# Attention cut into units of 32 queries and 64 keys: two transposes a block, sixteen small products each for scores and outputs, one tile of two banks

## The chip, the cores and the metric

The program runs on one core of one Trainium2 chip. The metric is device time in microseconds (us), the median of 3 runs. Engines are called as in the profile: PE is TensorE (PEld its weight loads), DVE is VectorE, ACT is ScalarE, POOL is GpSimd, SP is SyncE, which here issues most of the loads.

## The reference, cut to what matters

Three stages follow each other: attention with two kinds of mask, a chain of four products, and a mixture of 8 experts to which tokens are assigned in order of their logits. The change touches the attention alone.

```python
# q, k, v: (4, 8, 576, 64), f32
scores = q @ k.T / sqrt(64)
rel = pos[:, None] - pos[None, :]
# heads 0..3: 0 <= rel < 32;  heads 4..7: 0 <= rel < 128 and rel % 4 == 0
scores = where(mask, scores, -1e9)
attn = exp(scores - max); attn = attn / (sum + 1e-9)
x = attn @ v                                  # (2304, 512)
x = (((x @ w1) * (x @ w2)) @ w3) @ w_out
logits = x @ w_gate                           # then each token to one expert, 288 a expert
out[tokens of e] = relu(x @ e_w1[e]) @ e_w2[e]
```

A query sees 32 keys at most. For heads 4 to 7 the launch sorts positions by their remainder of 4, and then these heads have the same band of 32 keys.

## The kernel before

**Blocks.** The attention runs over 36 blocks, 9 for each of 4 batches (`NB`). A block is 64 queries of each of 8 heads with the 96 keys that they can see. In blocks 0 to 7 of a batch all 64 queries belong to one stretch of positions; the ninth (`t % 9 == 8`) collects what is left over of the sorted heads, with its own mask and extra keys and values (`ke`, `ve`).

**One block on each engine.** `att_qk` makes the scores on PE: 8 products of 64 queries by 96 keys over 64 rows, into two banks of PSUM, one for even and one for odd heads (`par`). Every f32 product is two matmuls in the trace. `att_max` (DVE, L193) adds the mask and takes the maximum, four instructions of 128x96. `att_exp` (ACT, L200) makes four exponentials with their sums. `att_norm` divides (two small DVE instructions, then one POOL product of 128x384, L207). `att_tr` turns the block with four PE transposes (L213) into a bank called `tr`, `h` or `ab`; `att_pt` copies it out (ACT, L217). `att_av` makes the outputs with 8 products of 96 keys (L228, in the ninth block also L231) into the bank `rt`. `att_out` writes the rounded value `xh` (two ACT copies, L251 and L252) and the rest `xl` (two DVE subtractions, L253 and L254).

**What runs beside it.** `moe(b)` makes the two products of a batch with w1 and w2 (L477 to L479, three matmuls for each f32 pair, 12 to a product), and `narrow12` and `narrow3` turn the 64-bit weights into f32 on DVE (L135, L137, L139), ACT (L121) and POOL (L124). The attention is a generator; the loop at the end of the listing pulls a step of it after so many dozens of matmuls (`ATT_RATE`, `RUSH`, `FIRST`), so the order of every engine's instructions is fixed by this code. Each engine takes its instructions in order.

**Two phases.** Up to block 17 (`ALONE`) a step of the generator is a single block: the PE gets, without a matmul of `moe` between them, the transposes of block t-2, the outputs of block t-3 and the scores of block t+1. From block 18 on a step takes two blocks: outputs of two, transposes of two, scores of two, then 36 matmuls of `moe`. Batch b needs the blocks of its own eight full positions; the ninth blocks of all batches go into `XT`, which batch 3 reads first.

**Tiles.** PSUM has 8 banks: 4 `ab` (the accumulators of `moe`), 2 `h`, 1 `tr`, 1 `rt`. The scores of the first 7 blocks take `ab` and their transposes `h`; later scores take `h`. A tile is given out again when all that read it are done. Loads: `qk_load` (320 KB a block) is issued three to four blocks ahead, `v_load` (192 KB) one ahead, both by SP, with the 1 MB weight loads in the same row. Eight semaphores stand for the loads in turn, so a load waits until the eighth before it has landed.

Of the kernel before, what the change touches and what calls it, by code (L numbers as in the profile page):

```python
# [21 lines left out]
QB, KB, NB = 64, 96, 9  # L22
HT = 288
# [64 lines left out]
def body(tc, qk_d, v_d, ke_d, ve_d, msk_d, cst_d, tri_d, w1_d, w2_d, w3_d, wo_d, wg_d, e1_d, e2_d, out):  # L88
    nc = tc.nc
    stacks = {}  # L90

    def pool(name, **kw):
# [4 lines left out]
    ps = pool("ps", space=PSUM)  # L97
    wp = pool("wp")
# [4 lines left out]
    bank = lambda shape, tag, dt=F32: ps.tile(shape, dt, tag=tag, name="ps_" + tag,  # L103
                                              bufs={"ab": 4, "h": 2, "tr": 1, "rt": 1}[tag])
# [39 lines left out]
    msk = pa.tile([128, 3, KB], F32, name="msk")  # L144
# [14 lines left out]
    def v_load(t):  # L159
        V[t] = pa.tile([KB, 512], F32, tag="v", name="v", bufs=4)  # L160
        nc.sync.dma_start(V[t], v_d[t // NB, t % NB])
        if t % NB == NB - 1:
            VE[t] = pa.tile([KB, 256], F32, tag="ve", name="ve", bufs=1)
            nc.sync.dma_start(VE[t], ve_d[t // NB])

    def att_qk(t, s=None):
        x = QK.pop(t)
        q = x[:, :256].rearrange("p (i q) -> p i q", i=4)
        k = x[:, 256:].rearrange("p (i q) -> p i q", i=4)

        s = SC[t] = s or [bank([128, 2, KB], "h" if t >= EARLY else "ab") for _ in range(2)]
        ke = KE.pop(t, None)
        for j in range(2):
            for par in range(2):
                r = slice(par * 64, par * 64 + 64)
                for i in (2 * j, 2 * j + 1):
                    p0 = i % 2 * 64
                    if ke is None or j == 0:
                        mm(s[par][p0:p0 + 64, j, :], q[r, i, :], k[r, i, :], start=True, stop=True)
                        continue  # L180
                    for a, key in enumerate((k[r, i, :], ke[r, i - 2, :])):
                        mm(s[par][p0 + 32 * a:p0 + 32 * a + 32, j, :], q[r, i, 32 * a:32 * a + 32], key,
                           start=True, stop=True)

    def att_max(t):
        s = SC.pop(t)
        j = t % NB
        m = 2 if j == 8 else int(j < 4)
        p = pa.tile([128, 4, KB], F32, tag="p", name="p", bufs=4)
        sm = pa.tile([128, 4, 4], F32, tag="sm", name="sm", bufs=4)  # L190
        for i in range(4):
            n = m if i % 2 else int(j == 0)
            dve.tensor_tensor_reduce(p[:, i, :], s[i // 2][:, i % 2, :], msk[:, n, :], scale=-0.125, scalar=1e9, op0=OP.add,  # L193
                                     op1=OP.min, accum_out=sm[:, 1, i:i + 1])
        P[t] = p, sm
# [7 lines left out]
    def att_norm(t):  # L203
        p, sm = P[t]
        dve.tensor_scalar(sm[:, 3], sm[:, 2], 1e-9, None, op0=OP.add)  # L205
        dve.reciprocal(sm[:, 3], sm[:, 3])
        nc.gpsimd.tensor_tensor(p, p, sm[:, 3, :, None].to_broadcast([128, 4, KB]), op=OP.mult)  # L207

    def att_tr(t, tag):
        p = P.pop(t)[0]  # L210
        o = TR[t] = bank([KB, 4, 128], tag)
        for i in range(4):
            nc.tensor.transpose(o[:, i, :], p[:, i, :], ident)  # L213

    def att_pt(t):
        pt = OT[t] = pa.tile([KB, 4, 128], F32, tag="pt", name="pt", bufs=2)
        act(pt, TR.pop(t), AF.Copy)  # L217

    def att_av(t, o=None):
        pt, v, ve = OT.pop(t), V.pop(t), VE.pop(t, None)  # L220
        o = AV[t] = bank([128, 4, QB], "rt") if o is None else o
        for i in range(4):
            for par in range(2):
# [3 lines left out]
                if ve is None or i < 2:  # L227
# [6 lines left out]
    def att_out(t):  # L234
# [11 lines left out]
        def dilated(x):  # L246
            if j == 8:
                return x[:, 2:4, w].rearrange("p h (i c) -> p h c i", c=4)
            return x[:, 2:4, t0:t0 + 253:4]
        od = o[:, 2:4].rearrange("p h (c i) -> p h c i", c=4) if j == 8 else o[:, 2:4]  # L250
        act(xh[:, 0:2, w], o[:, 0:2], AF.Copy)  # L251
        act(dilated(xh), od, AF.Copy)  # L252
        dve.tensor_tensor(xl[:, 0:2, w], o[:, 0:2], f32(xh)[:, 0:2, w], op=OP.subtract)  # L253
        dve.tensor_tensor(dilated(xl), od, dilated(f32(xh)), op=OP.subtract)  # L254

    def attention():

        for t in range(ALONE):
# [18 lines left out]
        qk_load(ALONE + 3)  # L277
        yield done - 1
# [3 lines left out]
        while done < NT:  # L282
            new = list(range(t, min(t + 2, NT)))
            t += 2
            if turned:
                o = bank([128, len(turned), 4, QB], "rt")
                for i, x in enumerate(turned):
                    att_av(x, o[:, i])
            for x, tag in zip(ready, ("tr", "ab")):
                att_tr(x, tag)  # L290
            if new:
# [3 lines left out]
                for x in (t + 2, t + 3):  # L295
                    if x < NT:
                        qk_load(x)
# [216 lines left out]
    nc.sync.dma_start(msk[:, :2], msk_d[:, :2])  # L514
# [6 lines left out]
    while nxt < 4:  # L521
# [4 lines left out]
        if i == 9:  # L526
            nc.sync.dma_start(msk[:, 2:], msk_d[:, 2:])
# [5 lines left out]
    for b in range(B):  # L533
        if b == 3:
            stacks.pop("pa").close()
            p2 = pool("p2")
# [623 lines left out]
    for name in ("p4", "p2", "pm", "xp", "wp", "ps", "dram", "cst"):  # L1160
# [58 lines left out]
```

## Time and profile before

| | |
|---|---|
| Median of 3 runs | 732.63 us (732.27 to 733.89) |
| Profiled execution | 730.56 us |
| its span | 728.8 us, 15964 instructions |
| PE busy in the span | 699.4 us (96%), mean granted clock 0.985 |
| DVE, ACT, POOL busy | 411.4 us, 352.7 us, 264.4 us |

The profiled execution is 1.76 us longer than its span and 2.07 us below the median. A row of the trace names the line of the kernel, the engine, the operation, the tile written and the tiles read, and the sizes; `xN` is the number of instructions that it stands for. Times of matmuls overlap: the start of the next row tells when PE went on, and the duration includes the way through the array.

### The profile page before, as it was taken

How to read it: one execution, taken by the hardware profiler on the slowest of the kernel's cores; microseconds unless marked ns; L12 is line 12 of the kernel's file. 1: busy time of each engine (PE TensorE's matmuls, PEld its weight loads, DVE VectorE, ACT ScalarE, POOL GpSimd, SP SyncE). 2: the span in 40 equal slices, each digit the busy share in tenths (PEclk: the TensorE clock that was granted, in tenths of full speed). 3: DMA queues.
4: the chain of work that ended last, by engine and by line, in shares of the span. 5: the costliest groups of instructions: out<-in, count | busy, mean ns of one | idle time of the engine just before them, and what ended most of it. 6: DMA issues, size and time to landing. Idle time of an engine off the chain costs nothing.

```text
span 728.8 us, 15964 instructions
## 1 busy us (share of the span) xinstructions
PE 699.4 (96%) x6081; PEld 608.9 (84%) x6081; DVE 411.4 (56%) x1414; ACT 352.7 (48%) x812; POOL 264.4 (36%) x305
## 2 busy tenths in 40 slices
PE   4799999999999999999999999999999999999996
PEld 3599778888889988687787878799999999999995
DVE  4879777773321011177886677779687862234321
ACT  5676444555422123333454565355565657655432
POOL 2858421321100035344445253421414145654521
PEclk9599999999999999999999999999999999999998
DMA  8995787971024300111799999768888898996311
GB/s 292 330 298 166 250 324 276 333 262 60 29 73 159 112 5 1 64 60 15 124 137 154 164 151 229 136 201 219 218 265 212 212 246 239 285 274 194 114 33 33
DMA packets 59596, 126.66 MB, mean 174 GB/s; under 512 B 13696, under 2 KB 29440, under 8 KB 56960
## 3 DMA queue, kind: packets, MB, share of 16 engines
q1 hardware_dynamic: 27232, 89.46, 37.0%
q0 software_dynamic: 29696, 31.46, 25.6%
q10 hardware_dynamic: 2592, 4.72, 1.9%
q8 instruction: 48, 0.79, 0.4%
q14 instruction: 28, 0.23, 0.1%
HBM read 87.87 MB, written 15.73 MB: 142 GB/s over the span
## 4 chain that ended last, share of the span: by engine, by line
PE 79%; DVE 7%; issue 6%; ACT 3%; POOL 3%; DMA 1%; POOLq 0%; SPq 0%; DVEq 0%; ACTq 0%
PE ps_ab L477 10%; PE ps_ab L478 9%; PE ps_ab L479 9%; PE ps_ab L623 4%; PE ps_h L1044 3%; PE ps_ab L624 3%; PE ps_ab L625 3%; PE ps_h L1045 3%; PE ps_h L1046 3%; PE ps_ab L1068 3%; PE ps_ab L1069 3%; PE ps_ab L1070 3%; PE ps_rt L821 3%; PE ps_rt L228 2%; PE ps_ab L592 2%
## 5 line engine op out<-in xcount | busy, mean ns | idle before, releaser
L207 POOL TENSOR_TENSOR p<-p,sm 128x384 f32<-128x384 f32 x36 | 45.7, 1280 | 120.5 <-DVE sm L205 74.4
L1068 PE MATMUL ps_ab<-hh,w 128*128 128x288 f32 x248 | 75.8, 306 | 0.0
L1070 PE MATMUL ps_ab<-hh,w 128*128 128x288 f32 x248 | 73.0, 294 | 0.0
L1069 PE MATMUL ps_ab<-hl,w 128*128 128x288 f32 x248 | 73.0, 294 | 0.0
L507 POOL DMA_DIRECT2D wbl<-g x36 | 48.4, 1675 | 63.1 <-ACT wbl L505 54.0
L1056 ACT ACTIVATE hh<-ps_h 128x288 fp32r<-128x288 f32 x62 | 25.6, 413 | 89.3 <-PE ps_h L1046 82.2
L1057 DVE SCALAR_TENSOR_TENSOR hl<-ps_h,hh 128x288 fp32r<-128x288 f32 x62 | 28.3, 456 | 64.7 <-ACT hh L1056 57.0
L200 ACT ACTIVATE p<-p,sm 128x96 f32<-128x96 f32 x144 | 52.0, 363 | 24.8 <-DVE sm L193 23.9
L482 ACT ACTIVATE a<-ps_ab 128x512 f32<-128x512 f32 (+1 forms) x44 | 22.9, 522 | 81.7 <-PE ps_ab L479 74.0
L623 PE MATMUL ps_ab<-Wx,wbh 128*128 128x512 f32 x144 | 59.7, 415 | 0.0
L624 PE MATMUL ps_ab<-Wx,wbh 128*128 128x512 f32 x144 | 56.3, 391 | 0.0
L625 PE MATMUL ps_ab<-Wx,wbl 128*128 128x512 f32 x144 | 56.2, 390 | 0.0
L477 PE MATMUL ps_ab<-x,wah 128*128 128x512 f32 (+1 forms) x144 | 54.8, 381 | 0.7 <-ACT x L251 0.7
L477 PE MATMUL ps_ab<-x,wbh 128*128 128x512 f32 (+1 forms) x144 | 54.5, 378 | 0.0
L478 PE MATMUL ps_ab<-x,wah 128*128 128x512 f32 (+1 forms) x144 | 53.4, 370 | 0.1
L479 PE MATMUL ps_ab<-x,wal 128*128 128x512 f32 (+1 forms) x144 | 53.2, 370 | 0.0
L478 PE MATMUL ps_ab<-x,wbh 128*128 128x512 f32 (+1 forms) x144 | 53.2, 369 | 0.0
L479 PE MATMUL ps_ab<-x,wbl 128*128 128x512 f32 (+1 forms) x144 | 53.2, 369 | 0.0
L484 DVE TENSOR_TENSOR g<-a,ps_ab 128x512 f32<-128x512 f32 (+1 forms) x36 | 22.4, 624 | 53.5 <-PE ps_ab L479 50.6
L1068 PEld LDWEIGHTS ps_ab<-hh,w 128*128 128x128 f32 x248 | 46.8, 189 | 0.0
L1069 PEld LDWEIGHTS ps_ab<-hl,w 128*128 128x128 f32 x248 | 46.7, 188 | 0.1
L1070 PEld LDWEIGHTS ps_ab<-hh,w 128*128 128x128 f32 x248 | 46.5, 188 | 0.0
(296 smaller groups left out, 2041.2 us busy)
## 6 DMA issues: line engine op xcount, KB each, us to landing
est<-e_dram SPq DMA_DIRECT2D x53, 512.0 KB, 5.5
w<-w_dram SPq DMA_DIRECT2D x16, 1024.0 KB, 9.0
qk<-qk_dram SPq DMA_DIRECT2D x36, 320.0 KB, 4.1
w<-est POOLq DMA_DIRECT2D x20, 512.0 KB
wbl<-g POOLq DMA_DIRECT2D x28, 256.0 KB
v<-v_dram SPq DMA_DIRECT2D x36, 192.0 KB, 6.8
kept<-f SPq DMA_DIRECT2D x12, 512.0 KB, 4.8
rows<-e_dram SPq DMA_DIRECT2D x11, 512.0 KB, 4.5
```

The costliest lines, as they stand in the source:

```text
L200: act(p[:, i, :], p[:, i, :], AF.Exp, bias=sm[:, 1, i:i + 1], scale=-1.0, accum_out=sm[:, 2, i:i + 1])
L207: nc.gpsimd.tensor_tensor(p, p, sm[:, 3, :, None].to_broadcast([128, 4, KB]), op=OP.mult)
L477: mm(a, wh[:, k, fs], xh[:, k, ts], start=(k == 0), stop=False)
L478: mm(a, wh[:, k, fs], xl[:, k, ts], start=False, stop=False)
L479: mm(a, wl[:, k, fs], xh[:, k, ts], start=False, stop=(k == 3))
L507: nc.gpsimd.dma_start(x, src, accum_op=OP.add)
L623: mm(a, h[:, f, :], wh, start=(f == 0), stop=False)
L624: mm(a, h[:, f, :], wl, start=False, stop=False)
L625: mm(a, l[:, f, :], wh, start=False, stop=(f == 7))
L1068: mm(y, wh[:, f % 2, ds_], h, start=(f == 0), stop=False)
L1069: mm(y, wh[:, f % 2, ds_], l, start=False, stop=False)
L1070: mm(y, wl[:, f % 2, ds_], h, start=False, stop=(f == end))
```

## The change

A block of 64 queries and 96 keys becomes two units of 32 queries and 64 keys (`UQ`, `UK`): unit u has the queries 32u to 32u+31 and the keys 32u to 32u+63 of the block. The ninth block of a batch stays as it was, with 96 keys.

- Scores: 16 products of 32 queries by 64 keys in place of 8 of 64 by 96. The four head pairs stand in four groups of 32 partitions, the unit in the free dimension.
- Mask, exponentials and division work on 128x64 and 128x256 in place of 128x96 and 128x384.
- Two transposes of 128x128 in place of four of 128x96; the copy `pt` is 128x256 in place of 96x512.
- Outputs: 16 products over 64 keys, 32 columns each, in place of 8 over 96 keys with 64 columns. Unit u uses the keys' rows 64u to 64u+63 and writes bank u.
- The banks `tr` and `rt` become one tile of two banks (`ps_t`, one buffer) that holds the outputs of one or two blocks and the transposes of one or two others. The outputs stand ahead of the transposes on PE in the single steps too. Transposes no longer use `h` and `ab`. From batch 3 on the two banks are `tr` and `rt` again (`psb`).
- The values of a block are loaded by two loads of 64 rows (128 KB each) in place of one of 96 rows; the mask by four small loads that ACT issues and two POOL copies.
- From block 18 on the ninth block (26 and 35) has a step for itself, so there is one step more.

```diff
-    bank = lambda shape, tag, dt=F32: ps.tile(shape, dt, tag=tag, name="ps_" + tag,
-                                              bufs={"ab": 4, "h": 2, "tr": 1, "rt": 1}[tag])
+    def bank(shape, tag, dt=F32):
+        return (psb if tag in ("tr", "rt") else ps).tile(shape, dt, tag=tag, name="ps_" + tag,
+                                                         bufs={"ab": 4, "h": 2, "tr": 1, "rt": 1}[tag])
...
+    def mask_loads():
+        for g in range(4):
+            nc.scalar.dma_start(mku[UQ * g:UQ * g + UQ, 0:2], msk_d[:UQ, 0:2, :UK])
+        for g in range(2):
+            nc.gpsimd.tensor_copy(mku[64 * g:64 * g + 64, 2], mku[64 * g:64 * g + 64, g])
...
     def v_load(t):
-        V[t] = pa.tile([KB, 512], F32, tag="v", name="v", bufs=4)
-        nc.sync.dma_start(V[t], v_d[t // NB, t % NB])
-        if t % NB == NB - 1:
+        V[t] = pa.tile([128, 512], F32, tag="v", name="v", bufs=4)
+        if not last(t):
+            for u in range(2):
+                nc.sync.dma_start(V[t][UK * u:UK * u + UK], v_d[t // NB, t % NB][UQ * u:UQ * u + UK])
+        else:
+            nc.sync.dma_start(V[t][:KB], v_d[t // NB, t % NB])
...
+        if not last(t):
+            for u in range(2):
+                for i in range(4):
+                    for par in range(2):
+                        r = slice(par * 64, par * 64 + 64)
+                        mm(s[par][UQ * i:UQ * i + UQ, u, :UK], q[r, i, UQ * u:UQ * u + UQ], k[r, i, UQ * u:UQ * u + UK],
+                           start=True, stop=True)
+            return
...
+    def turn_bank():
+        return psa.tile([128, 2, 512], F32, tag="t", name="ps_t", bufs=1)
...
-        o = TR[t] = bank([KB, 4, 128], tag)
-        for i in range(4):
-            nc.tensor.transpose(o[:, i, :], p[:, i, :], ident)
+        o = TR[t] = o[:, u, 256:].rearrange("p (x q) -> p x q", x=2)
+        for i in range(2):
+            nc.tensor.transpose(o[:, i, :], p[:, 2 * i:2 * i + 2, :].rearrange("p u k -> p (u k)"), ident)
...
+        if not last(t):
+            o = AV[t] = o[:, :, 128 * n:128 * n + 128].rearrange("p u (i q) -> p u i q", i=4)
+            for i in range(4):
+                for u in range(2):
+                    for par in range(2):
+                        h = 2 * i + par
+                        mm(o[par * 64:par * 64 + 64, u, i, :], v[UK * u:UK * u + UK, h * 64:h * 64 + 64],
+                           pt[UK * u:UK * u + UK, par, UQ * i:UQ * i + UQ], start=True, stop=True)
+            return
...
             if t >= 2:
-                att_tr(t - 2, "tr" if t - 2 >= EARLY else "h")
+                o = turn_bank()
+                if t >= 3:
+                    att_av(t - 3, o)
+                att_tr(t - 2, o)
                 att_pt(t - 2)
-            if t >= 3:
-                att_av(t - 3)
             v_load(t + 1)
...
-            new = list(range(t, min(t + 2, NT)))
-            t += 2
-            if turned:
-                o = bank([128, len(turned), 4, QB], "rt")
+            new = list(range(t, min(t + (1 if last(t) else 2), NT)))
+            t += len(new)
+            if turned or ready:
+                o = turn_bank()
                 for i, x in enumerate(turned):
-                    att_av(x, o[:, i])
-            for x, tag in zip(ready, ("tr", "ab")):
-                att_tr(x, tag)
+                    att_av(x, o, i)
+                for i, x in enumerate(ready):
+                    att_tr(x, o, i)
...
-    nc.sync.dma_start(msk[:, :2], msk_d[:, :2])
+    mask_loads()
```

The order of instructions on PE, first at a single step (outputs of block 7, transposes of block 8 are told by their counts; names are tiles, `C` the identity matrix, `pt` the turned block), before and then of the change:

```order
L479 MATMUL ps_ab<-x,wbl 128x256
L213 MATMUL ps_tr<-C,p 96x128 x4
L228 MATMUL ps_rt<-pt,v 64x64 x8
L179 MATMUL ps_h<-qk 64x96 x8
L477 MATMUL ps_ab<-x,wah 128x256
```

```order
L533 MATMUL ps_ab<-x,wbl 128x256
L266 MATMUL ps_t<-pt,v 64x32 x16
L247 MATMUL ps_t<-C,p 128x128 x2
L195 MATMUL ps_h<-qk 32x64 x16
L531 MATMUL ps_ab<-x,wah 128x256
```

The outputs now stand first, so the transposes no longer run ahead of them; both write the one tile `ps_t`.

On PE where a step takes two blocks (outputs of 18 and 19 and what follows them), before and then of the change:

```order
L479 MATMUL ps_ab<-x,wal 128x512
L228 MATMUL ps_rt<-pt,v 64x64 x16
L213 MATMUL ps_tr<-C,p 96x128 x4
L213 MATMUL ps_ab<-C,p 96x128 x4
L179 MATMUL ps_h<-qk 64x96 x16
L477 MATMUL ps_ab<-x,wbh 128x512
```

```order
L533 MATMUL ps_ab<-x,wal 128x512
L266 MATMUL ps_t<-pt,v 64x32 x32
L247 MATMUL ps_t<-C,p 128x128 x4
L195 MATMUL ps_h<-qk 32x64 x32
L531 MATMUL ps_ab<-x,wbh 128x512
```

The order is the same here; the counts are doubled for the products and halved for the transposes.

On PE at the end of the attention (`xt` is what the ninth blocks write), before: the outputs of the last blocks, then 30 matmuls of batch 2 with 512 columns, of which the first stands here, and only then `xt` is read:

```order
L228 MATMUL ps_rt<-pt,v 64x64 x12
L231 MATMUL ps_rt<-pt,v 64x32
...
L231 MATMUL ps_rt<-pt,ve 64x32
L477 MATMUL ps_ab<-x,wbh 128x512
L478 MATMUL ps_ab<-x,wbh 128x512
```

and of the change:

```order
L277 MATMUL ps_t<-pt,v 64x64 x4
L280 MATMUL ps_t<-pt,v 64x32
...
L280 MATMUL ps_t<-pt,ve 64x32
L531 MATMUL ps_ab<-xt,wah 128x256
L532 MATMUL ps_ab<-xt,wah 128x256
```

The outputs of block 35 have moved behind all of batch 2, and the first matmul after them reads `xt`, to which they belong.

## Rows read from the trace of the kernel before

**Rows 1.** The page: busy time and instructions by engine; PE's instruction queue q8.

```profile
PE 699.4 (96%) x6081; PEld 608.9 (84%) x6081; DVE 411.4 (56%) x1414; ACT 352.7 (48%) x812; POOL 264.4 (36%) x305
...
q8 instruction: 48, 0.79, 0.4%
```

**Rows 2.** Two stretches: length, busy us of PE, PEld, DVE, ACT, POOL, clock, DMA share.

```profile
28.90:104.50 75.60, 72.55 (x798) 62.14 (x796) 60.46 (x194) 42.93 (x161) 41.65 (x40) 0.96 0.81 262
104.50:213.50 109.00, 108.87 (x994) 88.59 (x994) 60.47 (x238) 51.03 (x196) 21.74 (x18) 1.00 0.51 177
```

**Rows 3.** PE's waits: who, for whom; us in total, times, longest.

```profile
PE ps_ab L179 <- DMA qk<-qk_dram: 9.7, 5, 4.0
PE ps_h L179 <- ACT pt L217: 2.4, 2, 1.8
```

**Rows 4.** PE in time, one step of two blocks: start, duration, what.

```profile
121.68 1.15 PE L228 MATMUL ps_rt<-pt,v 96*64 96x64 f32 x32
122.76 0.64 PE L213 MATMUL ps_tr<-C,p 128*96 128x128 f32 x4
123.24 0.60 PE L213 MATMUL ps_ab<-C,p 128*96 128x128 f32 x4
123.77 0.89 PE L179 MATMUL ps_h<-qk 64*64 64x96 f32 x32
124.59 0.50 PE L477 MATMUL ps_ab<-x,wbh 128*128 128x512 f32 x1
```

**Rows 5.** PE in time, scores of a ninth block: matmuls of 64*32 tiles.

```profile
80.78 0.27 PE L182 MATMUL ps_h<-qk 64*32 64x96 f32 x1
...
80.83 0.27 PE L182 MATMUL ps_h<-ke,qk 64*32 64x96 f32 x1
80.89 0.24 PE L182 MATMUL ps_h<-qk 64*32 64x96 f32 x1
...
81.10 0.50 PE L477 MATMUL ps_ab<-x,wah 128*128 128x512 f32 x1
```

**Rows 6.** PE in time, the last outputs, with products of 32 columns.

```profile
211.66 0.39 PE L478 MATMUL ps_ab<-x,wbh 128*128 128x512 f32 x1
211.88 0.39 PE L479 MATMUL ps_ab<-x,wbl 128*128 128x512 f32 x1
212.20 0.92 PE L228 MATMUL ps_rt<-pt,v 96*64 96x64 f32 x24
212.95 0.31 PE L231 MATMUL ps_rt<-pt,v 96*64 96x32 f32 x4
...
213.54 0.50 PE L477 MATMUL ps_ab<-x,wbh 128*128 128x512 f32 x1
```

**Rows 7.** PE in time, a single step; in brackets its wait.

```profile
59.53 0.60 PE L213 MATMUL ps_tr<-C,p 128*96 128x128 f32 x4
60.38 0.69 PE L228 MATMUL ps_rt<-pt,v 96*64 96x64 f32 x16 [0.25 <-PE ps_tr L213]
```

**Rows 8.** DVE in time, beside that step.

```profile
59.89 0.39 DVE L254 TENSOR_TENSOR x<-ps_rt,x 128x128 fp32r<-128x128 f32 x1
```

**Rows 9.** ACT and DVE in time, after the last outputs.

```profile
213.65 0.28 ACT L251 ACTIVATE x<-ps_rt 128x128 fp32r<-128x128 f32 x1 [2.10 <-PE ps_rt L231]
...
214.45 0.38 DVE L254 TENSOR_TENSOR x<-ps_rt,x 128x128 fp32r<-128x128 f32 x1
```

**Rows 10.** DMA queues and issues of the first 60 us: packets, size, us to landing.

```profile
DMA packets 6151, 17.48 MB, mean 291 GB/s; under 512 B 992, under 2 KB 1600, under 8 KB 5120
...
v<-v_dram SPq DMA_DIRECT2D x14, 192.0 KB, 9.3
```

**Rows 11.** A stretch at the lower clock, columns as in rows 2.

```profile
35.20:38.50 3.30, 3.30 (x32) 2.85 (x29) 3.02 (x14) 1.94 (x10) 2.55 (x3) 0.50 1.01 331
```

**Rows 12.** PE in time there: 12 matmuls of 256 columns and what follows.

```profile
35.87 0.58 PE L477 MATMUL ps_ab<-x,wbh 128*128 128x256 f32 x1
...
38.60 0.60 PE L213 MATMUL ps_h<-C,p 128*96 128x128 f32 x4
```

More of the change, by code (lines that the diff above doesn't have):

```diff
@@ L141, in steps64, with last @@
         yield
-    msk = pa.tile([128, 3, KB], F32, name="msk")
+    msk = pa.tile([128, 2, KB], F32, name="msk")
+    mku = pa.tile([128, 3, UK], F32, name="mku")
+    def mask_loads():
[3 more added lines that the diff above has]
+            nc.gpsimd.tensor_copy(mku[64 * g:64 * g + 64, 2], mku[64 * g:64 * g + 64, g])
+    def last(t):
+        return t % NB == NB - 1
     C = cst.tile([128, C_END], F32, name="C")
@@ L187, in att_max @@
         j = t % NB
-        m = 2 if j == 8 else int(j < 4)
-        p = pa.tile([128, 4, KB], F32, tag="p", name="p", bufs=4)
+        w = KB if last(t) else UK
+        p = pa.tile([128, 4, w], F32, tag="pw" if last(t) else "p", name="p", bufs=1 if last(t) else 4)
         sm = pa.tile([128, 4, 4], F32, tag="sm", name="sm", bufs=4)
         for i in range(4):
-            n = m if i % 2 else int(j == 0)
-            dve.tensor_tensor_reduce(p[:, i, :], s[i // 2][:, i % 2, :], msk[:, n, :], scale=-0.125, scalar=1e9, op0=OP.add,
+            m = msk[:, i % 2] if last(t) else mku[:, 0 if i % 2 or j >= 4 else 2 if j else 1]
+            dve.tensor_tensor_reduce(p[:, i, :], s[i // 2][:, i % 2, :w], m, scale=-0.125, scalar=1e9, op0=OP.add,
                                      op1=OP.min, accum_out=sm[:, 1, i:i + 1])
@@ L244, in att_out, with spots @@
         t0 = 256 * (j // 4) + j % 4
[L246 to L254, printed above, removed]
+        if last(t):
+            def spots(x):
+                return x[:, 0:2, w], x[:, 2:4, w].rearrange("p h (i c) -> p h c i", c=4)
+            ins = o[:, 0:2], o[:, 2:4].rearrange("p h (c i) -> p h c i", c=4)
+        else:
+            def spots(x):
+                return [y.rearrange("p h (u q) -> p h u q", u=2) for y in (x[:, 0:2, w], x[:, 2:4, t0:t0 + 253:4])]
+            ins = [o[:, :, i:i + 2].rearrange("p u i q -> p i u q") for i in (0, 2)]
+        for x, y in zip(spots(xh), ins):
+            act(x, y, AF.Copy)
+        for x, y, z in zip(spots(xl), ins, spots(f32(xh))):
+            dve.tensor_tensor(x, y, z, op=OP.subtract)
     def attention():
@@ L294, in attention @@
                     att_qk(x, [y[:, i] for y in o])
-                for x in (t + 2, t + 3):
-                    if x < NT:
-                        qk_load(x)
+                while loaded < min(t + 4, NT):
+                    qk_load(loaded)
+                    loaded += 1
             yield done
@@ L526, in body @@
         if i == 9:
-            nc.sync.dma_start(msk[:, 2:], msk_d[:, 2:])
+            for n in range(2):
+                nc.sync.dma_start(msk[:, n], msk_d[:, 2 * n])
             nc.sync.dma_start(wg, wg_d)
@@ L1159, in body @@
         pass
-    for name in ("p4", "p2", "pm", "xp", "wp", "ps", "dram", "cst"):
+    for name in ("p4", "p2", "pm", "xp", "wp", "psb", "ps", "dram", "cst"):
         stacks[name].close()
```

32 lines of the change are left out of this document (24 added, 8 removed).

## The prediction

> **What bounds the kernel now.** I read the page's busy times first: PE works 699.4 of 728.8 us, DVE 411.4, ACT 352.7, POOL 264.4 [rows 1]. Then the stretches in which attention runs. From 104.5 to 213.5 us, where blocks go two to a step, PE is busy 108.87 of 109.00 us [rows 2]; nothing but PE time counts there, and what PE saves ends up in the total. From 28.9 to 104.5, with single blocks, PE is busy 72.55 of 75.60 us, but DVE 60.46 as well [rows 2]: PE's order is mostly the limit, and here and there it meets a late DVE. Before that the start is a chain with loads in it: PE waited 9.7 us in 5 waits for `qk`, and 2.4 us in 2 waits for the copy `pt` that frees a bank `h` [rows 3]. In the first 60 us the DMA engines move 291 GB/s [rows 10]; their busy share there is about full, 1.01 in the stretch of rows 11. After 213.5 us attention is over; the rest keeps its work and moves as one piece, so gains and losses carry over one to one.
>
> **The change part by part.** The unit is a step of two blocks: outputs from 121.68, transposes from 122.76 and 123.24, scores from 123.77, `moe` again at 124.59 [rows 4], together 2.91 us.
>
> *Transposes.* The second four make the stretch 0.48 us longer (123.24 less 122.76) [rows 4]. Four of eight go: -0.48 us a step of two, -0.24 a block.
>
> *Scores.* Two blocks are 32 matmuls now, four side by side, and take 0.82 us [rows 4]; less 0.17 us from the last start to the next work (80.93 is the last start, 81.10 the next row) [rows 5] that is 8 rounds of 0.08 us for 96 columns. They become 64 matmuls in 8 rounds of eight. The ninth block has this shape, 64*32: eight start within 0.05 us (80.78 to 80.83), the second eight 0.11 us after the first [rows 5]. With 64 columns a round should take two thirds of 0.08, 0.055 us, just above the 0.05 in which eight start. Then 0.11 + 6 x 0.055 + 0.05 + 0.17 = 0.66 us, -0.16 a step; at 0.11 a round, the one gap that the trace has for eight, 0.99 us, +0.17. I take -0.16, since four rounds side by side go at 0.08 with more columns.
>
> *Outputs.* 32 matmuls, two side by side, take 1.08 us [rows 4]: less 0.15, 16 rounds of 0.058 us. The products of 32 columns in the last outputs take 0.59 us for 16 (212.95 to 213.54) [rows 6], 8 rounds of 0.055: half the columns save nothing. The change has 64 matmuls, four side by side, again 16 rounds. I take 0; from -0.05 up to +0.35, if a round of four takes the 0.08 us of the scores.
>
> So a step of two loses 0.64 us, 2.91 to 2.27. After 104.5 us there are 8 pairs of transposes and 7 of scores left: 8 x -0.48 + 7 x -0.16 = **-4.9 us**.
>
> *The step more.* Blocks 26 and 35 ran with a neighbour; each now has runs of its own. A run of outputs, transposes and scores more costs three times the 0.15 to 0.17 us in which nothing starts, and 0.09 for going from `moe` to outputs (0.32 us from 211.88 to 212.20 in place of 0.22) [rows 6]: **+0.6 us**.
>
> *The last block.* The outputs of block 35 now stand right ahead of the matmuls that read `xt`. After the last outputs PE could go on at 213.54 [rows 6]; ACT began at 213.65 and DVE ended the second subtraction at 214.83 [rows 9]. Of these 1.3 us a first matmul of 0.12 fills something, and it needs ACT's copies alone: 0.4 to 1.2 us, **+1.1 us** taken, for the second matmul needs what DVE writes. What hid this before were 30 matmuls of batch 2.
>
> *Single steps.* Two transposes fewer and half of the scores' gain are -0.32, the extra change from `moe` to outputs +0.09: -0.23 us a step. Six such steps lie between 61.6 and 104.5: -1.4. But outputs, now first, wait for the tile that the block before has not left: one buffer, which DVE's subtraction ends. At 59.53 PE had transposes to do and then waited 0.25 us for DVE's L254, which ended at 60.28 [rows 7, 8]; now the transposes stand behind that wait, and such a step gets 0.2 to 0.3 us longer. Two of the four steps from 46 to 61.6 are like that, which leaves 0 for these four. For the six later ones I count half of the gain, **-0.7 us** (0 to -1.4), since DVE is busy 80% there [rows 2].
>
> *Loads.* A block's values come in two loads of 128 KB in place of one of 192. Of 14 in the first 60 us [rows 10] 12 are ordinary blocks: 0.8 MB, at 291 GB/s 2.7 us of DMA time where DMA is full; behind each extra load on SP stand `qk` and the weight loads, and scores wait for `qk`. Against that, the two waits on `h` (2.4 us) [rows 3] lose their cause, as transposes leave `h`, and exponentials, masks, the POOL product and the copy shrink by a third to a half. I take **+0.3 us**, from -3.8 (below) to +2.7. Later loads have time: PE shows no wait on them. Mask loads on ACT and the POOL copies lie ahead of the first scores, at zero; ACT and DVE have nothing else to do then.
>
> *More instructions.* 12162 PE instructions come in 48 packets of q8 [rows 1], 253 each; an ordinary block gets 60 more, 1920 in all, 7.5 packets. A step of two now has 264 within 2.3 us, more than a packet holds. A packet takes about 0.97 us (0.4% of 16 engines' span, by 48) [rows 1]. No row before shows what a late one costs: 0 to 7.5 x 0.97 = 7.3 us; **+0.4 us** taken, near 0, because a step of two has 144 today (72 matmuls, each with a weight load) and shows no gap [rows 4].
>
> Sum: -4.9 + 0.6 + 1.1 - 0.7 + 0.3 + 0.4 = -3.2 us. The profiled execution would go from 730.56 to 727.4 us, the median, 2.07 us above it, from 732.63 to 729.4.
>
> **The rivals.**
>
> *Small matmuls don't go side by side as hoped (slower).* Rounds of eight take 0.11 us and rounds of four 0.08. Then a step of two stays at 2.95 us: 8 x -0.48 + 7 x 0.17 + 8 x 0.35 = +0.2 in place of -4.9, and the six single steps +0.1 each in place of -0.7 together. Sum +3.2, 735.8 us. It decides from the step's length: above 2.9 us the change loses. For it: no row has more than two rounds of eight in a row. Against: eight start within 0.05 us [rows 5].
>
> *Each small matmul pays for itself, one after the other.* The 16 products of 32 columns start on average 0.028 us apart; if that were the price of every instruction, a block would take 64 x 0.028 + 0.3 = 2.1 us for scores and outputs in place of 0.95, and 22 blocks would add some 20 us: 750 us. Eight starts within 0.05 us speak against it [rows 5]. [...]
>
> *Instructions come late (slower).* Each of the 7.5 packets more stops PE for its 0.97 us: +6.9 on the sum, 736.3 us.
>
> *The loads take the start (no change).* +2.7 in place of +0.3: -0.8, 731.8 us. It shows as longer waits of the scores on `qk`.
>
> *The start gives more (faster).* Both waits on `h` vanish (-2.4), and with them the lower clock: after the longer of them the clock was 0.50, 1.2 GHz, from 35.2 to 38.5 [rows 11], and 12 matmuls took 2.73 us (35.87 to 38.60) [rows 12]; at full clock half, -1.4. Together -3.8 in place of +0.3: -7.3, 725.3 us. Against it: PE would then arrive earlier at loads that come later.
>
> **How the numbers follow.** Forecast 0.52, late start gains 0.09, loads 0.18, rounds 0.12, packets 0.07, serial price 0.02. Below 0.2% (1.5 us, about what a measurement can tell from none) lie forecast and start gains nearly whole: faster 0.60; same 0.19; slower 0.21. The range, 725.5 to 734.5 us, takes in the start's gain nearly whole, the loads, and part of the rounds' and packets' rivals; it leaves out about 0.06 below and 0.14 above.
>
> **What would show it.** A step of two, from its first outputs to `moe`, at 2.27 us; four transposes at 0.5; scores of two blocks at 0.66 and outputs at 1.08. At the end of batch 2 a wait of about 1.1 us ahead of the first matmul on `xt`, put down to ACT or DVE. Outputs of single steps waiting for DVE near 50 and 60 us. Waits on `qk` near 9.7 us. The prediction is wrong if the step of two is above 2.6 us, if stops of about 1 us lie inside such steps, or if batch 0 begins more than 2 us later than 28.9 us, where the first stretch of rows 2 begins.

## The result, and the profile after

The changed kernel takes 738.4 us (median of 18 runs), the kernel before, in the same session, 732.2 (18 runs): ratio 1.0062, interval 1.0041 to 1.0084. (Single runs spread over 8 to 9 us; the two means stand at 1.0065, the two medians at 1.0085. The ratio is what is compared below.) It is slower; 729.4 us had been predicted, from 725.5 to 734.5. The profiled execution took 735.88 us, its span is 734.1, against 728.8 before.

The page of the changed kernel, as in [rows 1]. PE has 5.4 us less work in a span that is 5.3 us longer: the work went as intended, the waiting grew by twice that.

```profile
PE 694.0 (95%) x7041; PEld 601.6 (82%) x7041; DVE 402.3 (55%) x1414; ACT 343.3 (47%) x812; POOL 253.9 (35%) x307
...
q8 instruction: 55, 0.90, 0.5%
```

The stretches of [rows 2], cut at the first `moe` of batch 1 and behind the last outputs; columns as there. The first holds the same work as before and now lasts 81.5 us in place of 75.6, with PE busy 73.0 in place of 72.6. The second, 113.5 us, is full of PE work; it holds 30 `moe` matmuls more than before, since the last outputs now stand behind them.

```profile
28.90:110.40 81.50, 73.04 (x1166) 60.57 (x1158) 57.37 (x195) 40.65 (x163) 40.35 (x41) 0.99 0.84 261
110.40:223.90 113.50, 113.11 (x1441) 91.39 (x1441) 60.54 (x242) 47.37 (x201) 15.20 (x18) 0.99 0.54 179
```

So the loss lies ahead of 110 us. PE in time, at the start of the same `moe` matmuls in both traces (counted from the first): number 1 at 28.9 before and 29.1 after, number 25 at 40.4 and 40.5, number 73 at 52.0 and 55.9, number 259 at 94.2 and 96.9, number 289 at 104.5 and 110.4, number 313 at 113.3 and 119.1, and the first transposes of `wo` behind attention at 224.8 and 228.8. Against the kernel before nothing is lost up to 40 us, and 4 us between 40 and 56; 1.3 come back by 97; 3.2 go at 104.5; 1.8 come back in the steps of two.

PE's waits in the first 60 us of the changed kernel, as [rows 3], and below them its wait at 104.5 us: who, for whom; us in total, times, longest. `qk` rose from 9.7 to 12.6 us; all but 0.5 of that, and the wait for DVE's L306, lie ahead of 29 us.

```profile
PE ps_ab L195 <- DMA qk<-qk_dram: 12.1, 4, 4.4
PE ps_ab L195 <- DVE x L306: 2.5, 1, 2.5
...
PE ps_t L266 <- ACT x L304: 1.1, 1, 1.1
...
PE ps_h L195 <- DMA qk<-qk_dram: 0.5, 1, 0.5
```

```profile
PE ps_t L243 <- POOL p L232: 3.1, 1, 3.1
```

The wait at 104.5 us, by the chain of work that ended last (start, us, what), from the outputs of block 14 on. Behind the outputs stand two loads of values (L177), one of `qk` (L168) and a store (L411) on SP; only then the last load of `wo` goes out, at 91.92, and takes 10.62 us to land. DVE works in order: the conversion of that weight (L140), the maxima of block 18 (L218), then the reciprocals of block 17 at 106.2 us; POOL's product and PE's transposes of block 17 wait for those. Before, the same load left at 88.08, and DVE waited for it as well (1.25 us, up to 96.16), but that early PE still had other work to do: POOL's product of block 17 ended at 101.88 us, and the transposes began at 101.93.

```profile
88.76 0.60 PE ps_t L266 x32
...
89.93 0.70 SPq L177
...
90.67 0.58 SPq L168
...
91.36 0.52 SPq L411
...
91.92 10.62 DMA w<-wo_dram
...
104.41 1.12 DVE f L140
105.54 0.13 DVE p L218
```

Behind that wait the granted clock stood at 0.50 of full speed for 3.4 us (columns as in [rows 2]), right where PE had transposes, scores and `moe` to catch up with; before, it was full (1.00) from 39 to 700 us.

```profile
108.40:111.80 3.40, 3.32 (x71) 2.31 (x71) 1.41 (x8) 2.24 (x11) 0.00 (x0) 0.50 1.05 340
```

PE in time, a step of two blocks, the counterpart of [rows 4]. It takes 2.44 us in place of 2.91: outputs 1.07 (1.08 before), transposes 0.58 (1.01), scores 0.79 (0.82).

```profile
127.44 1.14 PE L266 MATMUL ps_t<-pt,v 64*64 64x32 f32 x64
128.51 0.66 PE L247 MATMUL ps_t<-C,p 128*128 128x128 f32 x4
129.09 0.86 PE L195 MATMUL ps_h<-qk 64*32 64x64 f32 x64
129.88 0.50 PE L531 MATMUL ps_ab<-x,wbh 128*128 128x512 f32 x1
```

PE in time behind the last outputs, the counterpart of [rows 6, 9]; its wait in brackets. The products with `xt` wait for ACT's copies and then for DVE's subtraction, as the prediction had it.

```profile
223.87 0.39 PE L531 MATMUL ps_ab<-xt,wah 128*128 128x256 f32 x1 [0.37 <-ACT xt L304]
224.49 0.39 PE L532 MATMUL ps_ab<-xt,wah 128*128 128x256 f32 x1 [0.23 <-DVE xt L306]
```

The loads of the first 60 us, as [rows 10]; q1 is the queue of SP's loads: packets, MB, share of the 16 DMA engines' time. Before, that line was 6144, 17.39, 92.8%.

```profile
q1 hardware_dynamic: 6389, 17.47, 95.9%
...
v<-v_dram SPq DMA_DIRECT2D x25, 128.0 KB, 7.6
```

### The profile page after: what moved, and what is told of

The parts are those of the page before. It is cut to its first block, busy times and chain, and to the rows that moved or that the text cites. A ratio compares the mean times of both kernels' runs of the same rounds, so it can differ in the third digit from the quotient of the medians.

```text
span 734.1 us, 17890 instructions
## 1 busy us (share of the span) xinstructions
PE 694.0 (95%) x7041; PEld 601.6 (82%) x7041; DVE 402.3 (55%) x1414; ACT 343.3 (47%) x812; POOL 253.9 (35%) x307
## 3 DMA queue, kind: packets, MB, share of 16 engines
q1 hardware_dynamic: 28768, 91.51, 38.8%
## 4 chain that ended last, share of the span: by engine, by line
PE 73%; DMA 8%; issue 6%; DVE 6%; POOL 3%; ACT 2%; SPq 1%; POOLq 0%; DVEq 0%; ACTq 0%
PE ps_ab L531 9%; PE ps_ab L532 8%; PE ps_ab L533 8%; PE ps_ab L680 4%; PE ps_ab L681 3%; PE ps_ab L682 3%; PE ps_h L1101 3%; PE ps_h L1102 3%; PE ps_h L1103 3%; PE ps_ab L1125 3%; PE ps_ab L1126 3%; PE ps_ab L1127 3%; PE ps_rt L878 2%; PE ps_ab L649 2%; PE ps_ab L651 2%
## 5 line engine op out<-in xcount | busy, mean ns | idle before, releaser
L232 POOL TENSOR_TENSOR p<-p,sm 128x256 f32<-128x256 f32 (+1 forms) x36 | 34.5, 967 | 136.9 <-ACT p L225 67.3
L1114 DVE SCALAR_TENSOR_TENSOR hl<-ps_h,hh 128x288 fp32r<-128x288 f32 x62 | 28.2, 455 | 64.7 <-ACT hh L1113 55.1
L225 ACT ACTIVATE p<-p,sm 128x64 f32<-128x64 f32 (+1 forms) x144 | 48.6, 340 | 25.2 <-DVE sm L218 25.2
L681 PE MATMUL ps_ab<-Wx,wbh 128*128 128x512 f32 x144 | 56.3, 391 | 0.0
```

The source lines that it names most:

```text
L225: act(p[:, i, :], p[:, i, :], AF.Exp, bias=sm[:, 1, i:i + 1], scale=-1.0, accum_out=sm[:, 2, i:i + 1])
L681: mm(a, h[:, f, :], wl, start=False, stop=False)
```

## Experiments

Ratios are to the kernel before, timed beside each kernel; its median was 729.99 to 733.94 us in these sessions, so ratios are compared and not medians. Traces show one execution of each kernel.

**A wait that the diff doesn't show.** ACT's waits from 28 to 60 us in the changed kernel have a row that has no like before: the copy that hands outputs on waits three times for PE's `moe` matmuls.

```profile
ACT x L304 <- PE ps_ab L533: 3.6, 3, 1.6
```

In the order of ACT's instructions, where each one's waits stand behind it, the second L304 of blocks 5, 6 and 7 has `[waits PE]`; before, its counterpart L252 has none. `moe` reads columns 0 to 255 of the tile then, and the copy writes 256 to 511, so nothing asks for that wait but the way in which the target is written: as 2 x 32 columns, in place of 64. The experiment writes it as before.

```
-return [y.rearrange("p h (u q) -> p h u q", u=2) for y in (x[:, 0:2, w], x[:, 2:4, t0:t0 + 253:4])]
+return [x[:, 0:2, w], x[:, 2:4, t0:t0 + 253:4]]
```

> The changed kernel; only the target of the four copies and subtractions that hand a block's outputs on is written as one run of 64 in place of 2 x 32, so that the second copy on ACT (L304) no longer carries a wait on PE. Theory A (that wait): in the changed kernel ACT stood 1.4 to 1.6 us before this copy in three blocks of batch 0, in each until 12 moe matmuls were over; outputs of the next block waited for the tile, and from 40.5 to 55.9 us PE fell 4.3 us behind the kernel before. Without the wait the idle row of L304 on PE is gone, moe after the ninth block's scores begins at 51.9 to 52.5 us in place of 55.9, and the time is 738.4 - 4.3 = 734.1 us if the wait of 3.1 us at 104.5 us stays, 731 if that one goes with it. Theory B (loads: 64 KB and one load more for each block hold the first 60 us): nothing changes, 738.4 us within 0.8, and PE's lag appears at other waits. Theory C (outputs ahead of transposes in one tile cost these 4.3 us without any false wait): ACT's row is gone, but PE still lags by more than 2.5 us at the moe matmuls of 55.9 us; 736.5 to 738.5 us.

Measured: ratio 1.0079 (1.0047 to 1.0110). ACT's row is gone, but no time came back that the intervals show. PE's waits in the first 60 us fit that: what was a wait for the tile is now a wait for `qk`, 15.8 us together.

```profile
PE ps_ab L195 <- DMA qk<-qk_dram: 13.3, 5, 4.3
PE ps_h L195 <- DMA qk<-qk_dram: 2.5, 2, 1.6
```

The other way round, the same wait put into the kernel before (the source of the copy is written alike):

```
-return x[:, 2:4, t0:t0 + 253:4]
+return x[:, 2:4, t0:t0 + 253:4].rearrange("p h (u q) -> p h u q", u=2)
```

> The kernel before; only the target of its second copy on ACT (L252) and second subtraction is written as 2 x 32 in place of 64, the same elements in the same order. The copy then carries a wait on PE in blocks 5, 6 and 7 of batch 0, as in the changed kernel. Theory A: the wait of 1.4 to 1.6 us shows on ACT three times; the outputs of the block after wait for the bank rt, and PE loses 1 to 4.3 us: 733.2 to 736.5 us against 732.2. Theories B and C: ACT waits, but PE has transposes to do first and the loads set the pace: 732.2 us within 0.8.

Measured: 1.0001 (0.9968 to 1.0034). ACT waited 2.2 us in two places for it, and the time stayed. Theory A falls as the cause of the change's loss.

**One load in place of two.** On top of e1_plain_write, the values are laid out by the host as the 128 rows that a block reads, and come in one load.

```
-for u in range(2):
-    nc.sync.dma_start(V[t][UK * u:UK * u + UK], v_d[t // NB, t % NB][UQ * u:UQ * u + UK])
+nc.sync.dma_start(V[t], v_d[t // NB, t % NB])
```

> The kernel of e1_plain_write, and a block's values are laid out for it as 128 rows and come in one load of 256 KB in place of two of 128: the same bytes, half the loads on SP. Theory A: the start needs neither, so within 1 us of e1_plain_write, at most 1.5 us better where the late load of wo at 92 us comes 0.5 us earlier behind one load less. Theory B in its form that the number of loads counts (SP's issue time and the load that must have landed before the next may go): 1.5 to 4 us below e1_plain_write; in its form that bytes count: equal to it, and both near 738.

Measured: 0.9954 (0.9920 to 0.9987), 1.25% below e1_plain_write, and below the kernel before. No theory had it so large. The first `moe` matmul starts at 26.2 us in place of 29.0, number 25 at 34.9 in place of 40.3, and PE's wait at block 17 shrinks from 2.3 to 1.0 us. More bytes were moved in the first 60 us in less of the DMA engines' time (17.64 MB and 95.2% in e1_plain_write):

```profile
q1 hardware_dynamic: 6824, 18.74, 85.3%
```

The clock differs as well. The twelve `moe` matmuls from 35.59 us in the changed kernel end with the row below, which starts 2.51 us after the first of them (from the second on one of 256 columns every 0.213 us, 1.2 columns a ns); for those from 40.46 it is 1.41. (The trace has no record of the clock there before 40.2.) In e3_plain_one_load the record begins at 31.2 us at full clock (1.00), after a start in which PE waited 7.8 us for `qk`; the second row (columns as in [rows 2]) is of that kernel. But the clock does not decide: matmuls 13 to 24 took 1.41 us in e9_two_loads_128_rows, which is slow, and 2.51 in e8_one_load_xt_later, which is fast (both below).

```profile
38.10 0.41 PE L533 MATMUL ps_ab<-x,wbl 128*128 128x256 f32 x1
```

```profile
31.30:35.00 3.70, 3.67 (x103) 2.94 (x103) 2.22 (x14) 3.04 (x17) 3.18 (x5) 1.00 1.01 396
```

**The same load in the changed kernel**, with the wait on PE left in (the diff is that of e3_plain_one_load alone):

> The changed kernel with the values in one load of 256 KB, as in e3_plain_one_load, and with the wait on PE that e1_plain_write took away. Theory B1 (loads alone decide, the wait on PE hides behind them): 727.4 us, as e3_plain_one_load, within 1. Theory A+B (both count, but in e1_plain_write the late qk took the place of the wait): 727.4 plus what the trace of the changed kernel lost between 40.5 and 55.9 us, 2 to 4.3 us: 729.4 to 731.7.

Measured: 0.9979 (0.9956 to 1.0001). Against the changed kernel's 1.0062 the load alone is worth 0.83%, 6.1 us (3.8 to 8.3, from both intervals). Between this and e3_plain_one_load lies 0.25%, which the intervals don't resolve; in the two traces `moe` matmuls 37 to 73 take 9.7 us with the wait and 8.2 without. Number 25 starts at 36.7 us, 3.7 ahead of the changed kernel, and number 73 at 50.6, 5.3 ahead. So more than half of what the two loads cost is lost by 40 us; against the kernel before that does not show, since with one load the units are 3.7 us ahead of it there. Of that lead 2.4 us go again up to number 73, with one load too.

**Units for the pairs alone**: blocks 0 to 17 are worked as before, and the units begin with block 18, with two loads for each block. The edit is a function `wide(t)`, true for `t < ALONE` and ninth blocks, in the places where the change asks for the ninth block; besides, the four loads of the small masks go out on SP at block 13, the two banks are joined at block 18, and the copies write as in e1_plain_write.

> Units of 32 queries and 64 keys only from block 18 on, where blocks go two to a step; blocks 0 to 17 are worked as in the kernel before (96 keys, four transposes, one load of values, transposes ahead of outputs, two banks). The small masks are loaded at block 13. All theories agree that the first 97 us are those of the kernel before. Theory A: nothing is lost before 104 us, and the pairs gain what the two traces show from 113 us on (the lag of the changed kernel shrinks from 5.8 us at 119.1 to 4.0 at 228.8): 732.2 - 1.8 = 730.4 us, 729.5 to 731.3. Theory D (the pairs are no gain, the shrinking lag is slack that only a late kernel can use): 732.2 us or more.

Measured: 1.0011 (0.9983 to 1.0038), no gain. A step of two takes 2.44 us here too, but PE waited for POOL at block 17, as in the changed kernel, and the clock fell behind that wait from 106.0 to 109.4 us, so the run does not tell what the pairs are worth by themselves. It shows that this wait comes without the two loads of 64 rows in the start (PE's waits from 62 to 125 us):

```profile
PE ps_t L251 <- POOL p L239: 2.0, 1, 2.0
```

**Number, bytes, place or rows?** Three kernels change the loads of the kernel before. First two loads of 48 rows in place of one of 96 (here and below the code is cut: ninth blocks keep their load):

```
-nc.sync.dma_start(V[t], v_d[t // NB, t % NB])
+for n in range(2):
+    nc.sync.dma_start(V[t][48 * n:48 * n + 48], v_d[t // NB, t % NB][48 * n:48 * n + 48])
```

> The kernel before; the values of a block (ninth blocks left as they are) come in two loads of 48 rows, 96 KB each, in place of one of 192 KB: the same bytes, one load more for each block on SP, nothing else changed. Theory B1 (the number of loads: a load on SP waits for the landing of the eighth before it, so a load more for each block leaves less ahead of the chain, and scores wait for qk): the start and the last single steps lose what e1_plain_write and e3_plain_one_load differ by, 735.5 - 727.4 = 8.2 us, perhaps half of it, since here no mask loads take places: 736 to 740 us against 731.9. Theory B2 (bytes): nothing changes, 731.9 us within 0.8.

Measured: 0.9995 (0.9972 to 1.0018): a load more for each block costs the kernel before nothing. Then 128 rows in one load, 32 of them, which the host adds, for nobody:

```
-V[t] = pa.tile([KB, 512], F32, tag="v", name="v", bufs=4)
-nc.sync.dma_start(V[t], v_d[t // NB, t % NB])
+V[t] = pa.tile([128, 512], F32, tag="v", name="v", bufs=4)
+nc.sync.dma_start(V[t], v_d[t // NB, t % NB])
```

> The kernel before; the load of a block's values fetches 128 rows, 256 KB, in place of 96 (the last 32 are read by nobody): 64 KB more for each block, the same number of loads. Theory B1: 731.9 us within 1, as there is room for the bytes. Theory B2 (bytes: 12 ordinary blocks in the first 60 us, 0.8 MB at 291 GB/s): up to 2.7 us slower, 733.5 to 734.6 us.

Measured: 1.0015 (0.9987 to 1.0042). More bytes cost nothing, since the engines needed less time for them than for 17.39 MB at 92.8%:

```profile
q1 hardware_dynamic: 6514, 18.17, 83.3%
```

It gained nothing either. PE's waits in its first 60 us: `qk` fell to 6.6 us, and POOL and DVE took the rest.

```profile
PE ps_ab L180 <- DMA qk<-qk_dram: 6.6, 3, 4.1
PE ps_h L214 <- POOL p L208: 3.6, 3, 1.4
PE ps_rt L230 <- DVE sm L194: 2.8, 3, 1.1
```

Third, the places of e6_before_256kb in memory, but 96 rows loaded of each (`v_d[t // NB, t % NB][:KB]`):

> The kernel before with its blocks of values 256 KB apart in memory, still loading 96 rows (192 KB) of each. e6_before_256kb loaded 128 rows from the same places and its DMA engines were busy 83.3% of the first 60 us for 18.17 MB, against 92.8% for 17.39 MB before. Theory address: share near 80%. Theory rows (96 rows fall unevenly on the engines and slow what runs beside them): near 93%. In both the time stays, 730 to 732 us, as e6_before_256kb showed no change.

Measured: 1.0009 (0.9973 to 1.0045), share 93.4% for 17.39 MB. Where the values lie in memory does not set the share.

On top of e3_plain_one_load: the same places and bytes, but two loads of 64 rows.

```
+nc.sync.dma_start(V[t][UK * u:UK * u + UK], v_d[t // NB, t % NB][UK * u:UK * u + UK])
```

> The kernel of e3_plain_one_load (values laid out as 128 rows for each block, 256 KB apart), but loaded in two pieces of 64 rows, as e1_plain_write does from blocks that lie 192 KB apart: the same bytes, and the addresses of e3_plain_one_load. In e1_plain_write 17.64 MB took 95.2% of the DMA engines' time in the first 60 us, in e3_plain_one_load 18.74 MB took 85.3%. Theory N (the number of loads, each of which holds one of eight places until it has landed): as e1_plain_write, 1.0079 of the kernel before, 735.5 us, PE waits some 15 us for qk, share near 95%. Theory R (where the values lie in memory, or how rows fall on the DMA engines): with the addresses changed alone, as e3_plain_one_load, 0.9954, 727 to 729 us, share near 85%, waits on qk near 8 us. In between means both.

Measured: 1.0052 (1.0020 to 1.0085): slow again, so places in memory are not it. Number or rows? In the same kernel two loads, each of all 128 rows and half of the columns:

```
+nc.sync.dma_start(V[t][:, 256 * u:256 * u + 256], v_d[t // NB, t % NB][:, 256 * u:256 * u + 256])
```

> The kernel of e3_plain_one_load with a block's values in two loads again, but each of all 128 rows and half of the columns (1 KB of a row) in place of 64 whole rows. Theory N (the number of loads): as e9_two_loads_128_rows, 1.0052 of the kernel before, waits of PE for qk 15 to 18 us in the first 62 us. Theory R (loads of fewer than 128 rows are slow for the DMA engines and for what runs beside them): as e3_plain_one_load, 0.9954, share of the engines near 87%, waits near 8 us; rows of 1 KB may cost a little of that.

Measured: 0.9937 (0.9906 to 0.9969), as fast as one load. The waits for `qk` did not come out as Theory R had it: 13.6 us, not 8. Two loads do bring the first `moe` matmul later, to 28.2 us; what follows is as in e3_plain_one_load, number 25 at 36.9 us (40.1 in e9_two_loads_128_rows). The rows of q1 tell the two apart, first of e9_two_loads_128_rows, then of e13_two_loads_all_rows:

```profile
q1 hardware_dynamic: 6232, 17.14, 97.1%
```

```profile
q1 hardware_dynamic: 8432, 18.20, 87.8%
```

So it is the rows of a load, not the number; Theory N falls. By the MB that q1 moved (share times 60 us, by MB) the engines took 2.7 to 2.9 us wherever an ordinary block's load fills all 128 partitions, and 3.0 to 3.4 wherever it fills 48, 64 or 96. The share alone does not part them so well: e4_units_from_18, which has the loads of the kernel before there, stands at 87.4%.

**Values later.** On top of e3_plain_one_load the values are loaded in the block's own step.

```
 qk_load(t + 3)
+if t:
+    v_load(t)
 ...
-v_load(t + 1)
```

> The kernel of e3_plain_one_load; a block's values are loaded in the block's own step, behind its load of q and k, in place of at the end of the step before. The buffer is then long free. Theory H (the loads of values stood on SP until PE had done the outputs of three blocks before, 16.2 us in the first 60 us of e3_plain_one_load, and the weight loads stood behind them): those waits shrink below 6 us, the last load of wo lands earlier, the wait of PE's transposes of block 17 on POOL near 100 us (3.1 us in the changed kernel, 1.0 to 2.7 with one load) goes: 727.4 - 1 to 3 = 724.4 to 726.4 us. Rival (the eight loads in flight set the pace whatever stands behind them): 727.4 us within 1.

Measured: 0.9916 (0.9883 to 0.9948). PE's wait for POOL at block 17 is gone; SP's loads of values still wait for PE, 12.4 us where it was 16.2, so that Theory H had that wait right, and not the way to it. The gain over e3_plain_one_load (0.38%) is inside the two intervals.

The kernel before with these loads, to see what the units are worth by themselves:

> The kernel before with the loads of e11_values_later: 128 rows, 256 KB for each block (32 of them read by nobody), loaded in the block's own step. e11_values_later stands at 0.9916 of the kernel before; what is left between the two is the units of 32 queries and 64 keys, with outputs ahead of transposes in one tile. Theory U (the units are worth what the prediction counted without loads, about 3.5 to 6 us): this kernel is at 0.9965 to 1.0015 of the kernel before, as e6_before_256kb. Rival (loads and their place were all of the gain): this kernel is at 0.992 too.

Measured: 1.0008 (0.9979 to 1.0037). With loads that are alike the units are worth 0.92%, 6.7 us (3.5 to 10, from both intervals).

**The order at `xt`, and everything together.** In batch 3, `todo = full[:1] + [(f, 3) for f in range(8)] + full[1:]`, on top of e3_plain_one_load:

> The kernel of e3_plain_one_load; in batch 3 the first f of the part that reads x goes ahead of the eight that read xt, so that 24 matmuls stand between the last block's outputs and the first reader of xt. The wait of 1.1 us after the last outputs (tail of the outputs 0.59 us, ACT and DVE after it) goes: 727.4 - 1.1 = 726.2 us, and the rows of waits on xt (0.4 on ACT, 0.2 on DVE) are gone. Rival: the loads of wo, which PE met late by 1.2 us in e3_plain_one_load, end the stage anyway, and PE waits for them: 727.4 us.

Measured: 0.9967 (0.9939 to 0.9994), no gain over 0.9954: the rival. The waits on `xt` are gone, and PE waits for the loads of `wo` instead, 2.2 us (1.2 in e3_plain_one_load).

```profile
PE ps_h L443 <- DMA wo<-kept: 2.2, 2, 2.0
```

Last, e11_values_later with this order and with the small masks in one load:

> The kernel of e11_values_later with the small masks laid out for one load of 96 KB on SP in place of four on ACT and two copies on POOL, and with the order of e8_one_load_xt_later in batch 3. The masks' four loads take four of the eight places at the start: C waited for them. Expected: 0.5 to 1.5 us earlier at the first moe matmul, and 1.1 us at xt: 723 to 725 us. Rival: both are hidden, as e11_values_later.

Measured: 0.9899 (0.9858 to 0.9941; 6 runs), the fastest here, 726.0 us where the kernel before took 731.3. It isn't told apart from e11_values_later; the first `moe` matmul starts 1.4 us earlier, at 26.5.

## Why the prediction was wrong

**Loads: the step that failed.** The prediction took +0.3 us, bound by +2.7, and reached that bound by dividing 0.8 MB by the 291 GB/s of [rows 10], as if the rate stayed. (13 of the 14 loads were ordinary blocks', not 12, which makes the bound 2.9.) It had read that the DMA engines were busy all the time (1.01 in [rows 11]), but not what their time was spent on. The two loads of 64 rows cost 6.1 us more than one of 128 (e7_changed_one_load against the change; 7 to 9 us in e1_plain_write against e3_plain_one_load and in e9_two_loads_128_rows against e3_plain_one_load and e13_two_loads_all_rows). That is more than the bound, and by a way that has no place in the sum: the engines work longer for the same bytes (3.29 us a MB in the changed kernel, 2.76 in e7_changed_one_load), and PE falls behind in the start. `moe` matmul number 73 begins at 54.6 to 56.3 us in the three kernels that begin with units and halves, and at 48.9 to 50.8 in the six with units and all rows. Which wait carries it is not shown: PE waited 12.6 us for `qk` in the changed kernel, but 13.6 in e13_two_loads_all_rows, which is fast. The rival "the loads take the start" named the place and had 0.18, but it ended at 731.8.

Why the DMA engines take longer over loads of 64 rows is not shown. The runs give the time (97.1% of the first 60 us for 17.14 MB in e9_two_loads_128_rows, 87.8% for 18.20 in e13_two_loads_all_rows); none shows how rows fall on the engines.

**The late weight at block 17.** That block's transposes stood within 0.1 us of a wait before; the prediction saw none and gave them no rival. It did say that behind each extra load on SP stand `qk` and the weight loads, and then asked only for the start what that costs ("later loads have time"). 3.2 us went here, part of it the clock. This is a second miss beside the loads, as their shape does not set it: the wait is 3.1 us in the changed kernel, but also 2.7 in e7_changed_one_load and 2.0 in e4_units_from_18, and 1.0 in e9_two_loads_128_rows and e3_plain_one_load alike. Only with the values loaded in the block's own step (e11_values_later, e12_all) do the units have none; what sets its length is open.

**The wait of ACT's copy.** The prediction treated the outputs' copies as moved, with the same waits. It was wrong on that, and the order would have shown it; the experiments show that it did not set the time of this change.

**Single steps: the gain right, the wait too small.** `moe` matmul number 121 (61.6 us before) lags by 3.7 us, number 259 by 2.7: five steps, 0.2 us gained in each, where the count had 0.23. The sixth met the late weight. The waits of outputs for the tile, forecast at 0.2 to 0.3 us behind DVE's subtraction, are longer: 1.1 and 1.5 us at 43 and 54 us in the changed kernel, there behind ACT's late copy. With the plain write and full loads the forecast wait itself shows, 1.4 us in e3_plain_one_load, e11_values_later, e12_all and e13_two_loads_all_rows: DVE subtracts only after a weight conversion of 1.52 us, and PE goes on 0.1 us after the subtraction (rows of e3_plain_one_load; "issue" means that the profile names no releaser). So with full loads the tile is late with ACT's wait and without it.

```profile
35.61 1.52 DVE L142 SCALAR_TENSOR_TENSOR f<-w,f 128x1024 int32<-128x1024 int32 x1
...
37.38 0.57 DVE L305 TENSOR_TENSOR x<-ps_t,x 128x128 fp32r<-128x128 f32 x2
...
38.06 0.67 PE L265 MATMUL ps_t<-pt,v 64*64 64x32 f32 x32 [1.44 <-issue]
```

**A step of two: right in kind, short in size.** Predicted 2.27 us, measured 2.44. Outputs 1.07 as forecast; transposes 0.58 for 0.53. The scores are the term that was mis-sized: 0.79 us, not 0.66. 64 matmuls in 8 rounds of eight start over 0.64 us, and the pace is uneven: the rounds begin at 0, 0.08, 0.14, 0.19, 0.27, 0.41, 0.48 and 0.55 us. Most stand 0.06 to 0.08 us apart, near the 0.055 that was taken, but the fifth, with which the second block begins, takes 0.15, and the last spreads over 0.09 in place of 0.05. So the gain is 0.03 a step in place of 0.16. Summed from `moe` matmul number 313 to the transposes of `wo`: transposes -2.8 us, scores -0.2, outputs with their wait +0.4, `moe` with its waits +0.8. Together -1.8, where -4.9 (unrounded -4.96) + 0.6 + 1.1 = -3.2 were forecast.

**The last block: right.** The first matmul on `xt` came 1.30 us after the first of block 35's outputs, which take 0.87 elsewhere, and the second 0.62 us behind it in place of 0.12: 0.9 us in all, 1.1 forecast. In e8_one_load_xt_later the wait is gone and PE waits 1.0 us longer for `wo` instead: it had covered that one.

**Instructions: no sign of them.** q8 grew by 7 packets, as counted, and the steps of two show no stop. The rival falls in that stretch, and with it the serial price, at 64 matmuls in 0.79 us (0.012 each); by its own terms that price was 22 x 1.15 = 25 us, not 20.

**Left open.** From the transposes of `wo` to the end the profiled execution of the changed kernel lost another 1.3 us (4.0 to 5.3), which no run here was made for. With equal loads the units are worth 6.7 us, where the terms without loads came to -3.5; that lies at the edge of the interval (3.5 to 10). The start, where PE then reaches the 25th `moe` matmul 2.2 us earlier (36.7 us in e11_values_later against 38.8 in e14_before_same_loads), is the part that the prediction gave to a rival ("the start gives more").

## What to carry to other kernels

- Where the DMA engines are busy all the time, ask what shape the loads have before dividing bytes by a mean rate: two loads of 64 rows cost 0.83% against one of 128 rows with the same bytes, and padding a load of 96 rows to 128 cost nothing that could be measured (e6_before_256kb, 1.0015).
- When a change makes the compute in a load-bound start shorter, look at the loads there again: their shape made no difference that could be measured to the kernel before, and 0.8 to 1.25% to the kernels with the units.
- List the waits of the new instruction order beside the old ones and look at each that is new, and at each step that stood close to waiting; here that shows ACT's copy and block 17.

## What the runs showed of the hardware that was not expected

The DMA engines' time went with how many partitions a load fills: 2.7 to 2.9 us a MB where a block's loads fill 128, 3.0 to 3.4 where they fill 48, 64 or 96. First 60 us: loads of values for an ordinary block, MB and share of q1, the engines' time by MB (share times 60 us, by MB), ratio of the kernel's time:

| kernel | load of a block's values | q1: MB, share | us a MB | ratio |
|---|---|---|---|---|
| before | 1 x 96 rows | 17.39, 92.8% | 3.20 | 1 |
| e4_units_from_18 | 1 x 96 rows | 17.39, 87.4% | 3.02 | 1.0011 |
| e10_before_256kb_apart | 1 x 96 rows, 256 KB apart | 17.39, 93.4% | 3.22 | 1.0009 |
| e5_before_two_loads | 2 x 48 rows | 17.39, 91.1% | 3.14 | 0.9995 |
| changed | 2 x 64 rows | 17.47, 95.9% | 3.29 | 1.0062 |
| e1_plain_write | 2 x 64 rows | 17.64, 95.2% | 3.24 | 1.0079 |
| e9_two_loads_128_rows | 2 x 64 rows, 256 KB apart | 17.14, 97.1% | 3.40 | 1.0052 |
| e6_before_256kb | 1 x 128 rows | 18.17, 83.3% | 2.75 | 1.0015 |
| e7_changed_one_load | 1 x 128 rows | 18.23, 84.0% | 2.76 | 0.9979 |
| e3_plain_one_load | 1 x 128 rows | 18.74, 85.3% | 2.73 | 0.9954 |
| e13_two_loads_all_rows | 2 x 128 rows, half the columns | 18.20, 87.8% | 2.89 | 0.9937 |

The loads beside them slow down too: the packets of 2560 bytes of `qk`, whose load is the same in every kernel, took 138 to 160 ns on average in the first seven of these kernels and 115 to 128 in the last four.

And eight matmuls of 64 x 32 tiles side by side begin a round with 64 columns every 0.06 to 0.08 us in most of a run of 64, with one gap of 0.15; four of 64 x 64 tiles with 96 columns take 0.08 a round ([rows 4]). The whole run was hardly shorter, 0.79 us in place of 0.82.
